# A gated long-convolution and token-mixer kernel on one core: spectral buffers laid out at equal steps, the filter's special row put last, a part of the first norm on ScalarE, a new order of the instructions

## The chip, the cores and the metric

The kernel runs on one core of one Trainium2 chip. A core has five engines that work side by side, each through its own instructions in order: TensorE (PE, matmuls, with weight loads shown as PEld), VectorE (DVE), ScalarE (ACT), GpSimd (POOL) and SyncE (SP). Here SP only issues transfers (DMAs), POOL issues some of them and computes a few reciprocal roots. Engines wait for each other by semaphores. The metric is the time of one execution on the device in microseconds (us), the median over several runs.

## The reference

All arrays are bf16. x is `A_q`, of 2048 tokens by 640 channels; k and v have the same shape.

```python
def _A_ref(q, k, v, shift_k, ssm_k, ssm_D):      # L = 2 * S
    k_shift = sum over t of k_pad[:, t:t + S] * shift_k[:, 3 - t]     # causal, four taps
    kv = k_shift * v
    y_f = rfft(kv padded to L) * rfft(ssm_k padded to L)
    y = irfft(y_f)[:, :S]
    return q * (y + kv * ssm_D)
def _B_ref(x, w1, w2, w3, w4):
    h = _gelu(_layernorm(x) @ w1)
    g0, g1, g2, g3 = quarters of h's channels, moved by +1, -1, +2, -2 tokens
    x1 = x + concat(g0, g1, g2, g3) @ w2
    return x1 + _gelu(_layernorm(x1) @ w3) @ w4            # w3: 640 x 1536
g = _sigmoid((x * gate_w).sum(-1))
return g * _A_ref(x, A_k, A_v, ...) + (1 - g) * _B_ref(x, w1, w2, w3, w4)
```

So there are two branches: a long convolution of every channel over 2048 tokens with a filter of 2048 taps (a circular one of length 4096, by a Fourier transform), and a mixer with two norms and four matrix products. A gate per token adds them.

## The kernel before, in words

**Recording, order, emission.** The kernel is written as functions that record operations (engine, what is read, what is written). `tt` (L661) is a DVE operation of two tensors, `ts` (L666) one of a tensor with scalars, `act` (L671) an ACT one, `mm` (L693) a chain of matmuls into one PSUM tile. Since such helpers record nearly everything, most instructions of the profile carry the helper's line. `scale` and `turn` (L678 to L686) choose between two engines for one operation: each call has a default, and a string `ON` of zeros and ones, one for each call, flips it. Which operation is issued when is not found by the program: `SEQUENCE` lists all 1163 operations by number in the order in which they are put into their engines' streams, and `PLACES` gives each of the 206 PSUM tiles its bank (there are 8). `emit` then derives the semaphore waits from what reads and writes the same memory. A stream is strictly in order: an instruction that waits holds up everything behind it on its engine.

**The convolution** works in five chunks of 128 channels, c = 0 to 4. The transform of length 4096 is split: tokens are laid out as n, 512 outer positions by matmul against fixed cosine and sine tables, and 4 blocks (b) of them that are combined as a short product of polynomials. For one chunk:

- `h_load`, `h_fold`: the filter is loaded, added to and subtracted from its own mirror (`add` and `sub`, 1024 elements a partition each), the skip weight `ssm_D` is added into the special element 0, and a DMA transpose ("T h") turns it by 128x128 blocks so that time lies on the partitions. `h_even`: sum and difference of its even part. Partition 0 holds a row that does not follow the rule of the others: two sums of one row on DVE and one scaled copy of one row correct it. `h_chunk`: the filter's spectrum, four matmul groups j = 0 to 3 into two PSUM banks each, each copied by ACT into the spectral buffer (`HF`).
- `k_load`, `v_load`: k and v come in by DMA transposes, so that channels lie on the partitions. `kv`: the four taps are scalings of k (2048 elements, by default 0, 1 and 3 on ACT and 2 on DVE), three shifted adds, the product with v, sum and difference with the mirror (a fold), and a DMA transpose ("T kv"). `kv2`: again sum and difference.
- `x_fwd`: the spectrum of kv, four groups j again, copied by ACT into `XF`. `combine`: two DVE operations across the blocks.
- `unit`: the product of the spectra, on DVE. Complex numbers are multiplied with three real products; `SX` is the sum of real and imaginary part of kv's spectrum, `HD` the sum and another buffer the difference for the filter's. For each output pair of blocks and each filter block a there is a product of 2 x 512 per block with two strides, another of 512 per block for the third, and an add into an accumulator. The sums of real and imaginary part (`Y`) are two subtractions or adds; a one-row copy fixes partition 0.
- `final(g, o, q, k)`: the inverse. Channels 0 to 383 are group 0 (chunks 0 to 2) and 384 to 639 group 1; there are eight calls of each, each for a pair of 128-token tiles. Two chains of matmuls, an ACT copy (`ab`), sum and difference on DVE (`gy`), a matmul against a flipped identity (`flip`) for the mirrored tile, its copy with the gate's weight, then product with q times gate, and the add to the mixer's output: group 0 by an accumulating DMA from POOL, group 1 by DVE from SBUF and a store by SP (64 KB stores for the last two calls of the function, 128 KB for the other six, in L1044 and after).

**The mixer** works in 16 tiles of 128 tokens, four to a superchunk (sc). `ln1`: mean and variance by DVE (`bn_stats`, L862, two halves a tile, and `bn_aggr`, L863) for tiles 0 to 9, by ACT (a sum and a sum of squares with an accumulator) for 10 to 15; a reciprocal root on POOL (L870); the application (subtract the mean, multiply) by DVE in all 16. Tiles 0 to 7 are then turned on PE (L923), the others by DMA transposes. `mm1` with gelu on ACT writes the hidden layer channels first; its fifth group of channels (`hx`) is moved by tokens in small copies on DVE or DMA (L947). `mm2` plus the residual is one DVE operation with an accumulated sum (L981), then ACT squares the tile for the second norm. `ln2` applies it (by default tiles 0 to 3 on DVE and the others on ACT), a DMA transpose follows. `mm3`, gelu, `mm4`; `base` scales half a tile by one minus the gate and stores it, and an accumulating DMA adds mm4's.

**What sets the order.** All streams interleave the two branches: PE goes from the first norm's transposes to mm1 of superchunks 0 to 2, chunk 0's filter matmuls (h, j = 0 to 3) between mm2 of the first tiles, and so on; the inverse comes last. Before the first real work PE runs 15 warm-up matmuls (L717) on a tile of ones, 512 columns each.

The five lines that place the first norm's split, which the change touches:

```python
PET, LNS, LNA = 8, 10, 4
...
            if t < LNS:
                ln_bn(t, X[:, t, :])
                continue
            act(xn1[t // 2 % 2][:, t % 2], X[:, t, :], ACTF.Copy, scale=1.0 / D, accum=bna[:, t, 0:1])
```

## Time and profile before

| | |
|---|---|
| median of 3 runs | 219.88 us (219.87 to 219.89) |
| span of the profiled execution | 218.0 us |
| PE busy | 208.8 us (96%) |
| PEld busy (lies beside PE) | 126.2 us (58%) |
| DVE busy | 211.7 us (97%) |
| ACT busy | 196.9 us (90%) |
| POOL busy | 46.5 us (21%) |
| DMA | 37.68 MB, mean 173 GB/s |

The profile is of one execution. Its span of 218.0 us runs from its first to its last instruction; what a run's time counts beyond that is the difference to the median, 1.9 us. A row of a group reads: line, engine, operation, what is written from what is read with the shape of each, how often, then busy time in all, mean nanoseconds of one, and idle time ahead of them with what ended most of it. A row of the timeline starts with its start and length in us; neighbours on one engine overlap a little, since an instruction starts before the one ahead has drained, so that the step from start to start is what one more instruction costs. Matmuls are pipelined too: a "busy" PE can also be one that waits for operands, so its busy share alone says little. "arena" is the one SBUF buffer in which the kernel places all its tiles.

### The profile page before, as it was taken

How to read it: one execution, taken by the hardware profiler on the slowest of the kernel's cores; microseconds unless marked ns; L12 is line 12 of the kernel's file. 1: busy time of each engine (PE TensorE's matmuls, PEld its weight loads, DVE VectorE, ACT ScalarE, POOL GpSimd, SP SyncE). 2: the span in 40 equal slices, each digit the busy share in tenths (PEclk: the TensorE clock that was granted, in tenths of full speed). 3: DMA queues.
4: the chain of work that ended last, by engine and by line, in shares of the span. 5: the costliest groups of instructions: out<-in, count | busy, mean ns of one | idle time of the engine just before them, and what ended most of it. 6: DMA issues, size and time to landing. Idle time of an engine off the chain costs nothing.

```text
span 218.0 us, 3825 instructions
## 1 busy us (share of the span) xinstructions
PE 208.8 (96%) x1400; PEld 126.2 (58%) x1410; DVE 211.7 (97%) x411; ACT 196.9 (90%) x328; POOL 46.5 (21%) x48
## 2 busy tenths in 40 slices
PE   6999999999999999999999999999999999999971
PEld 1699755554664446665446764446566445777740
DVE  5999999999999999999999999999999999999994
ACT  2699999999999999999999989999897977868882
POOL 0421103400001101000600301403004560256440
PEclk9999999999999999999999999999999999999995
DMA  5998799999999967999085684787289999069796
GB/s 158 348 242 224 182 220 226 219 202 246 298 228 197 353 172 150 191 195 203 29 162 99 123 201 96 71 180 126 72 123 164 176 206 265 5 74 103 80 165 136
DMA packets 79344, 37.68 MB, mean 173 GB/s; under 512 B 58969, under 2 KB 76894, under 8 KB 79326
## 3 DMA queue, kind: packets, MB, share of 16 engines
q1 hardware_dynamic: 73824, 31.86, 64.0%
q0 software_dynamic: 5328, 5.51, 19.1%
q8 instruction: 11, 0.18, 0.3%
q10 hardware_dynamic: 174, 0.07, 0.1%
q14 instruction: 7, 0.06, 0.1%
HBM read 14.88 MB, written 5.77 MB: 95 GB/s over the span
## 4 chain that ended last, share of the span: by engine, by line
PE 72%; DVE 17%; ACT 5%; DMA 3%; issue 2%
PE PSall L693 72%; DVE arena L661 8%; ACT arena L671 5%; DVE arena L862 4%; DVE arena L666 3%; DMA arena<-arena 2%; DVE arena L947 1%; DMA arena<-in_A_q_dram 1%; DVE arena L863 0%; DVE arena L737 0%; DVE arena L981 0%; DVE arena L867 0%
## 5 line engine op out<-in xcount | busy, mean ns | idle before, releaser
L693 PE MATMUL PSall<-arena 128*128 128x256 bf16 (+5 forms) x1339 | 201.1, 309 | 3.5 <-DVE arena L661 2.4
L661 DVE TENSOR_TENSOR arena<-arena 128x1024 bf16<-128x1024 bf16 (+11 forms) x264 | 174.3, 725 | 0.6
L693 PEld LDWEIGHTS PSall<-arena 128*128 128x128 bf16 x1349 | 121.9, 98 | 81.8 <-DVE arena L661 3.2
L671 ACT ACTIVATE arena<-PSall 128x512 bf16<-128x512 f32 (+7 forms) x158 | 94.9, 669 | 7.6 <-PE PSall L693 5.3
L671 ACT ACTIVATE arena<-arena 128x640 bf16<-128x640 bf16 (+6 forms) x107 | 94.1, 910 | 1.0 <-DMA arena<-arena 0.5
L870 POOL TENSOR_TENSOR arena<-arena 128x2 f32<-128x2 f32 (+2 forms) x15 | 17.6, 1174 | 92.9 <-DVE arena L867 78.2
L237 POOL DMA_DIRECT2D out_dram<-arena x24 | 24.7, 1235 | 37.6 <-ACT arena L671 19.8
L671 ACT ACTIVATE arena<-PSall,arena 128x640 bf16<-128x640 f32 (+2 forms) x32 | 20.6, 656 | 6.9 <-PE PSall L693 6.8
L981 DVE SCALAR_TENSOR_TENSOR arena<-PSall,arena 128x640 bf16<-128x640 f32 x16 | 13.0, 816 | 0.3 <-PE PSall L693 0.3
L237 POOL DMA_DIRECT2D arena<-arena x5 | 4.9, 988 | 35.5 <-DVE arena L661 28.4
L666 DVE TENSOR_SCALAR arena<-arena 128x640 bf16<-128x640 bf16 (+6 forms) x31 | 11.6, 385 | 0.1
L862 DVE BATCH_NORM_STATS2 arena<-arena 128x6 f32<-128x320 bf16 x20 | 8.6, 480 | 1.1 <-DMA arena<-in_A_q_dram 1.1
L717 PE MATMUL PSall<-arena 128*128 128x512 bf16 x15 | 6.7, 584 | 2.0 <-DVE arena L714 2.0
L947 DVE TENSOR_SCALAR arena<-arena 32x256 bf16<-32x256 bf16 (+1 forms) x24 | 5.8, 242 | 0.5
L671 ACT ACTIVATION_READ_ACCUMULATOR arena<-arena 128x1 f32 x28 | 6.2, 221 | 0.0
L717 PEld LDWEIGHTS PSall<-arena 128*128 128x128 bf16 x15 | 1.8, 129 | 4.2 <-issue 2.2
L923 PE MATMUL PSall<-arena 128*128 128x128 bf16 x40 | 3.5, 219 | 0.0
L671 ACT ACT_TABLE_LOAD x1 | 1.3, 1283 | 2.5 <-issue 2.5
L923 PEld LDWEIGHTS PSall<-arena 128*128 128x128 bf16 x40 | 2.8, 99 | 0.6 <-DVE arena L666 0.3
L867 DVE SCALAR_TENSOR_TENSOR arena<-arena 128x2 f32<-128x2 f32 (+2 forms) x19 | 2.8, 154 | 0.0
L863 DVE BATCH_NORM_AGGREGATE arena<-arena 128x2 f32<-128x12 f32 x10 | 1.7, 196 | 0.0
L981 DVE DVE_READ_ACCUMULATOR arena<-PSall,arena 128x1 f32 x16 | 1.3, 81 | 0.0
(21 smaller groups left out, 4.3 us busy)
## 6 DMA issues: line engine op xcount, KB each, us to landing
arena<-in_A_ssm_k_dram SPq DMA_DIRECT2D x5, 512.0 KB, 5.2
arena<-in_A_q_dram SPq DMA_DIRECT2D x6, 320.0 KB, 5.4
arena<-in_B_w_dram SPq DMA_DIRECT2D x1, 1920.0 KB, 9.0
out_dram<-arena SPq DMA_DIRECT2D x16, 96.0 KB, 2.5
arena<-arena POOLq DMA_DIRECT2D x4, 384.0 KB, 4.1
out_dram<-arena POOLq DMA_DIRECT2D x16, 96.0 KB, 4.5
arena<-in_A_q_dram SPq DMA_DIRECT2D x8, 192.0 KB, 4.0
out_dram<-arena POOLq DMA_DIRECT2D x8, 192.0 KB, 4.1
```

The source lines that it names most:

```text
L237: fn = lambda e: e.dma_start(out, in_, **kw)
L661: P.op(eng, lambda e: e.tensor_tensor(o, real(a), real(b), op), [a, b], [o], dve_ns(o, [a, b], 2) if eng == "dve" else 500)
L666: P.op(eng, lambda e: e.tensor_scalar(o, real(a), s1, s2, op0=op0, **({} if op1 is None else {"op1": op1})), [a] + aps, [o], dve_ns(o, [a] ...
L671: P.op("act", lambda e: e.activation(real(o), real(a), f, bias=bias, scale=scale, **({"accum_out": accum} if accum is not None else {})), ...
L693: fns.append(lambda e, l=l, r=r, i=i: e.matmul(real(o), l, r, start=(i == 0), stop=(i == last)))
L717: P.op("pe", lambda e: e.matmul(real(pw), warm[:, 0:128], warm[:, 128:640], start=True, stop=True), [warm], [pw], 427.0 if i < 14 else 216.0)
L862: P.op("dve", lambda e, o=o, i=i: e.bn_stats(o, i), [i], [o], 400)
L867: P.op("dve", lambda e: e.scalar_tensor_tensor(o, a, x, b, op0=op0, op1=op1), [a, b] + aps, [o], n_of(o) / 0.96 + 65)
L870: P.op("pool", lambda g: g.tensor_tensor(o, a, e, ALU.pow), [a, e], [o], dur)
L923: P.op("pe", [lambda e, c=c, pb=pb, xn=xn: e.transpose(real(pb)[:, 128 * c:128 * (c + 1)], xn[:, 128 * c:128 * (c + 1)], ident) for c in r ...
L947: P.op("dve", lambda e, o=hT[q, 4, c0:c0 + n], i=hx[q, :]: e.tensor_scalar(o, i, 1.0, None, op0=ALU.mult), [hx[q, :], hT[q, 4, c0 - 1:c0]] ...
L981: P.op("dve", lambda e: e.scalar_tensor_tensor(x, real(pr), 1.0, x, op0=ALU.mult, op1=ALU.add, accum_out=st[1, 0][:, t:t + 1]), [pr, x], [ ...
```

## The change

- **Spectral buffers at equal steps.** The real part, imaginary part and their sum of a chunk's spectrum (`oXr`, `oXi`, `oSX`) lie at one distance from each other, and the filter's difference, sum and real part (`oHm`, `oHP`, `oHr`) too. So the two sums SX and HP are one operation of 4096 elements, the two products of a step are one of 1536 per block (three strides), and the two halves of Y one subtraction.
- **The filter's special row last.** The tables are built so that the special element is the last of 128, not the first; `h_fold` writes plain blocks, and the two one-row sums and the one-row scaling of `h_even` are replaced by SP DMAs of one row: two copies in one operation, and a third that reads what the first writes. `copies` is new: several small DMAs counted on one semaphore.
- **First norm.** Statistics on ACT for tiles 1 and 10 to 15 (`SUMS`); application on ACT for 10 to 15 (`TURNS`), which needs one more small DVE operation (minus mean times root).
- **Unit's fix of one row.** A copy on ACT or two SP DMAs, by the switch.
- **Small things.** The warm-up reads one 128-column tile four times over instead of a 640-column one, its length in PSUM is the same; three small loads move from ACT's queue to POOL's; many buffers move; some constants of the planner's costs differ (they change no instruction).
- **New SEQUENCE, PLACES and ON.** There are now 1114 operations: DVE 352 instead of 395, ACT 283 instead of 302, SP 113 instead of 102, POOL 46 instead of 44, PE 320 as before. By the switches, ten instead of four taps run on DVE (0 and 1 of chunk 0; 0, 1 and 3 of chunk 1; 2 of chunk 0, 2 and 3; 0 and 3 of chunk 3; in chunks 1 and 4 tap 2 is on ACT), the second norm's application on DVE in tiles 0 to 3, 13 and 14, `base` on DVE in tiles 1, 2, 4, 12 and 14 instead of 5, and in the unit four adds instead of five go by DMA (u0 a=1, u1 a=2 and a=1, u2 a=1).

Some of what the new order puts where, since the prediction speaks of it:

- Loads of x on SP: tile 3, 0, 1, 2. On DVE: statistics of tiles 3 and 0, their aggregates, an epsilon of tile 3, the square of tile 1's mean (which reads ACT's sums), epsilon of tile 0, statistics of tile 2, variance of tile 1, application of tile 3, aggregate of tile 2, application of tile 0.
- ACT, a run of the stream: squares of tiles 2, 0, 3 (second norm), sums of 13 and 12 (first norm), square of 1, then 13, 15, 12, 14, a small copy, 15, 14, one gelu of hx (1024 tokens on), gelus of superchunk 2 groups 0 and 1, applications of tiles 13 and 12, gelus of groups 2 and 3, applications 14 and 15, then the copies of filter chunk 0, j = 0, 3, 2, 1, and the first forward copies.
- PE at that place: mm1 of superchunk 2, filter matmul c0 j = 2, 0, mm2 of tiles 7 and 9 in between, j = 3, and j = 1 into the bank of j = 3.
- SP in chunk 2: T h, load of w4, T of the second norm, the row's first two copies, T of the second norm, transpose of v, the row's last copy. The first PE user of the row is filter matmul c2 j = 3.
- DVE at the end: gy and ab sums, products and adds of the last calls of `final`; the last store on SP is the 128 KB one of call 5 in group 1.

```diff
+    def copies(self, queue, pairs):
+        fns = [lambda e, o=o, i=i: e.dma_start(o, i) for o, i in pairs]
+        op = Op(len(self.ops), queue, fns, [i for _, i in pairs], [o for o, _ in pairs], 470.0 * len(pairs), 0.0, 1024 * len(pairs))
+        op.cost = 10.0 * len(pairs)
+        op.lat = 2300.0
+        return self._record(op)
...
+    p = (np.arange(128)[:, None] + 1) % 128
...
+    xp = lambda i: oXF + U * (i + 2)
+    hp = lambda i: oHF + U * (i + 5)
+    XSTEP, HSTEP = (3, 4, 5, -1, 1), (1, 2, 3, 4, 5)
+    oXr, oXi = [xp(2 * i) for i in XSTEP], [xp(i) for i in XSTEP]
+    oHr, oHm = [hp(i) for i in HSTEP], [hp(-i) for i in HSTEP]
+    oSX, oHP, oTA, oRh = xp(0), hp(0), xp(7), xp(9)
...
-    P.op("dve", lambda e: e.memset(warm, 1.0), [], [warm], 230)
+    P.op("dve", lambda e: e.memset(warm, 1.0), [], [warm], 165)
+    wide = at_sb(oUT, (0, 4), (1, 128))
...
-    P.dma("act", shk5, A_shift_k.rearrange("(c p) j -> c (p j)", p=128))
+    P.dma("pool", shk5, A_shift_k.rearrange("(c p) j -> c (p j)", p=128))
...
     def h_even(c):
-
         ev, o = het[c], evn[c]
         tt(o[:, 0], ev[:, :, :, 0], ev[:, :, :, 1], ALU.add)
         tt(o[:, 1], ev[:, :, :, 0], ev[:, :, :, 1], ALU.subtract)
-        tt(o[0:1, 0, 0], ev[0:1, 1, :, 0], ev[0:1, 0, :, 0], ALU.add)
-        tt(o[0:1, 1, 0], ev[0:1, 1, :, 0], ev[0:1, 0, :, 0], ALU.subtract)
-        scale(o[0:1, :, 1], ev[0:1, :, :, 1], 1.0, True)
+        last = slice(127, 128)
+        P.copies(sp, [(ev[last, 1, :, 0], ev[last, 0, :, 0]), (ev[last, 1, :, 1], o[last, 1, 1])])
+        P.copies(sp, [(ev[last, 0, :, 0], o[last, 0, 1])])
...
-            if a >= LNS:
+            if a in SUMS:
                 tt(st[0, 4][:, a:b], mean, mean, ALU.mult)
                 stt(st[0, 3][:, a:b], st[0, 1][:, a:b], 1e-5, st[0, 4][:, a:b], ALU.add, ALU.subtract)
...
+            if a in TURNS:
+                stt(st[0, 6][:, a:b], mean, -1.0, st[0, 5][:, a:b], ALU.mult, ALU.mult)
...
+    SUMS, TURNS = (1, 10, 11, 12, 13, 14, 15), (10, 11, 12, 13, 14, 15)
...
-            ts(xn, x, bna[:, t, 0:1], st[0, 5][:, t:t + 1], ALU.subtract, ALU.mult)
+            if t in TURNS:
+                act(xn, x, ACTF.Identity, scale=st[0, 5][:, t:t + 1], bias=st[0, 6][:, t:t + 1])
+            else:
+                ts(xn, x, bna[:, t, 0:1], st[0, 5][:, t:t + 1], ALU.subtract, ALU.mult)
...
     def unit(c):
-        X4, H4 = XF[:, c], HF[c]
-        tt(SX, X4[:, :, 0], X4[:, :, 1], ALU.add)
-        tt(HD, H4[:, :, 0], H4[:, :, 1], ALU.add)
-        tt(H4[:, :, 1], H4[:, :, 1], H4[:, :, 0], ALU.subtract)
+        dx, dh = oXi[c] - oXr[c], oHP - oHm[c]
+        both = lambda x, h: at_sb(x, (h - x, 2), (1, U))
+        tt(both(oSX, oHP), both(oXr[c], oHr[c]), both(oXi[c], oHm[c]), ALU.add)
+        tt(V(oHm[c], U), V(oHr[c], U), V(oHm[c], U), ALU.subtract)
...
-                tt(to[:, :, 0:2], X4[:, x0:x0 + n], uv, ALU.mult)
-                tt(to[:, :, 2], SX[:, x0:x0 + n], H4[:, a, 0].unsqueeze(1).to_broadcast([128, n, 512]), ALU.mult)
+                tt(tmp if a else acc, at_sb(oXr[c] + 512 * (lo - a), (512, n), (dx, 3), (1, 512)),
+                   at_sb(oHm[c] + 512 * a, (0, n), (dh, 3), (1, 512)), ALU.mult)
...
-            tt(Y[:, :, 0], R[:, :, 2], R[:, :, 1], ALU.subtract)
-            tt(Y[:, :, 1], R[:, :, 2], R[:, :, 0], ALU.add)
-            scale(Y[0:1, :, :, 0:128], R[0:1, :, 0:2, 0:128], 1.0, True)
+            n = o1 - o0
+            tt(at_sb(oXr[c] + 512 * o0, (512, n), (dx, 2), (1, 512)), at_sb(oACC + 1024, (1536, n), (0, 2), (1, 512)),
+               at_sb(oACC + 512, (1536, n), (-512, 2), (1, 512)), ALU.subtract)
+            fix = lambda o, so, sr: bass.AP(AR[:, 0:16].tensor, o, [[part[0], 1], [so, n], [sr, 2], [1, 128]])
+            fo, fi = fix(oXr[c] + 512 * o0, 512, dx), fix(oACC, 1536, 512)
+            if turn(False):
+                P.copies(sp, [(fo[:, :, r], fi[:, :, r]) for r in range(2)])
+            else:
+                act(fo, fi, ACTF.Copy)
```

177 lines of the change are left out of this document (85 added, 92 removed), and 119 rows, old and new, of tables (PLACES, SEQUENCE).

## The prediction

> **What bounds the kernel now.** I read the page first (busy shares, slices), then the stretches by engine, then the groups by shape, then the timeline of each engine at three places.
>
> ```profile
> span 218.0 us, 3825 instructions
> PE 208.8 (96%) x1400; PEld 126.2 (58%) x1410; DVE 211.7 (97%) x411; ACT 196.9 (90%) x328; POOL 46.5 (21%) x48
> ```
>
> ```profile
> PE   6999999999999999999999999999999999999971
> ```
>
> ```profile
> DVE  5999999999999999999999999999999999999994
> ```
>
> ```profile
> 210.00:214.00 4.00, 1.57 (x11) 0.77 (x8) 4.00 (x16) 2.70 (x7) 1.20 (x1) 0.85 0.92 155
> ```
>
> The slices are tenths of 5.45 us each; the stretch from 210 to 214 us gives busy times of PE, PEld, DVE, ACT, POOL, then granted clock, DMA share and GB/s. PE and DVE are both full from 5 to 210 us; then PE runs dry and DVE does not. Is a full PE really working? The price of a matmul says so:
>
> ```profile
> L693 PE MATMUL PSall<-arena 128*128 128x512 bf16 x29 | 6.4, 379 | 0.0
> ```
>
> ```profile
> L693 PE MATMUL PSall<-arena 128*128 128x256 bf16 (+5 forms) x1339 | 201.1, 309 | 3.5 <-DVE arena L661 2.4
> ```
>
> ```profile
> 8.13 0.44 PE L923 MATMUL PSall<-arena 128*128 128x128 bf16 x5
> ```
>
> The first is the group row of 132 to 138 us: 0.22 us for 512 columns. The second is the page's row of all of this line, 201.1 us busy. The same by the price, in proportion to columns: 410 of 512, 264 of 384, 340 of 256, 160 of 320, 120 of 128 columns and 85 single ones make some 202 us. The third, of the timeline, is the first transpose, at 8.1 us; 202 from there end at 210. So PE loses about 1 us in 200, and its order cannot be fed late anywhere without moving the end. DVE is the second bound. Time by median is 219.88 us (219.87 to 219.89); the profiled execution has a span of 218.0, so I carry 1.9 us around it unchanged. Differences under 0.2% (0.44 us) I call no change.
>
> **The change, part by part.**
>
> *Work on each engine.* DVE prices:
>
> ```profile
> L661 DVE TENSOR_TENSOR arena<-arena 128x3072 bf16<-128x3072 bf16 x9 | 15.7, 1747 | 0.0
> L661 DVE TENSOR_TENSOR arena<-arena 128x1024 bf16<-128x1024 bf16 x89 | 58.2, 681 | 0.2
> L661 DVE TENSOR_TENSOR arena<-arena 128x2048 bf16<-128x2048 bf16 x39 | 47.0, 1214 | 0.1
> L661 DVE TENSOR_TENSOR arena<-arena 1x512 bf16<-1x512 bf16 x10 | 4.1, 405 | 0.0
> L666 DVE TENSOR_SCALAR arena<-arena 128x640 bf16<-128x640 bf16 x16 | 6.8, 428 | 0.0
> L666 DVE TENSOR_SCALAR arena<-arena 128x2048 bf16<-128x2048 bf16 x4 | 2.9, 748 | 0.0
> L671 ACT ACTIVATE arena<-arena 128x2048 bf16<-128x2048 bf16 x16 | 32.0, 2026 | 0.0
> L671 ACT ACTIVATE arena<-arena 1x1024 bf16<-1x1024 bf16 x4 | 4.2, 1039 | 0.0
> ```
>
> ```profile
> 3.44 1.67 DVE L862 BATCH_NORM_STATS2 arena<-arena 128x6 f32<-128x320 bf16 x4 [1.14 <-DMA arena<-in_A_q_dram]
> 5.03 0.33 DVE L863 BATCH_NORM_AGGREGATE arena<-arena 128x2 f32<-128x12 f32 x2
> ```
>
> 1024 and 2048 elements cost 681 + 1214 = 1895 ns apart and 1747 merged, of which neighbours overlap by some 80 ns: 0.07 us for each of 47 merges, -3.2. The ten 1-row sums of the filter go: -3.4 (0.405 less overlap). Six norm applications go to ACT, tile 1's statistics too (the two last rows: 0.42 each for two halves, 0.17 for the aggregate): -3.1. Against it the new switches put six more taps (0.67 each, +4.0), six second-norm applications (+2.1), six scalings of 0.2 and one add of 0.9 (+2.2) on DVE; small ones balance. Net about -2 us. ACT loses what these switches give DVE (six taps at 1.9, six applications, six scalings and an add) and the four filter copies at 1.0, and gains six first applications and some sums: about -17 us. PE keeps every matmul. Nothing of this shows unless PE's order is fed earlier; PE has only its front and its tail to give. The merged patterns I price as plain ones: today's product already walks two buffers by a stride at the price above. Its bounds are that price and, if merged, never under one of 2048.
>
> *The tail: -0.6 us.* Both orders end PE with equal work, so the last inverse is copied at the same moment, 210.79 + 0.60 = 211.4:
>
> ```profile
> 210.79 0.60 ACT L671 ACTIVATE arena<-PSall 128x512 bf16<-128x512 f32 x1
> ```
>
> ```profile
> 215.19 0.29 DVE arena L661
> ```
>
> ```profile
> L661 DVE TENSOR_TENSOR arena<-arena 128x512 bf16<-128x512 bf16 x17 | 6.9, 419 | 0.0
> L661 DVE TENSOR_TENSOR arena<-arena 128x256 bf16<-128x256 bf16 x24 | 6.3, 284 | 0.2
> ```
>
> Now DVE's last op ends at 215.5, after flips that PE does for it one by one. The new order has eleven DVE ops left (eight of 256 at 0.20 start to start, two of 512 at 0.34, one of 768 at 0.47): 2.8 us after 211.55, so 214.4, or 1.1 earlier. But its last store is of 128 KB instead of 64:
>
> ```profile
> out_dram<-arena SPq DMA_DIRECT2D x6, 128.0 KB, 2.6
> out_dram<-arena SPq DMA_DIRECT2D x4, 64.0 KB, 1.7
> ```
>
> 0 to 0.9 later; I take 0.5. Tail -0.6 (-1.1 to -0.2): 219.3 if nothing else happens.
>
> *Tile 1 of the first norm: DVE +1.2 us.* Its sums now come from ACT, and the product of means (m2 of tile 1) stands on DVE behind tiles 3 and 0 and ahead of tile 2's statistics. Tile 1 is the third load.
>
> ```profile
> 0.75 2.32 SPq L237 DMA_DIRECT2D arena<-in_A_q_dram  x5
> ```
>
> ```profile
> 0.75 2.66 DMA arena<-in_A_q_dram
> ```
>
> ```profile
> arena<-in_A_q_dram SPq DMA_DIRECT2D x4, 160.0 KB, 3.2
> ```
>
> ```profile
> 6.82 0.39 DVE L666 TENSOR_SCALAR arena<-arena 128x640 bf16<-128x640 bf16 x1
> ```
>
> ```profile
> 30.56 0.72 ACT L671 ACTIVATE arena<-arena 128x640 bf16<-128x640 bf16 x1
> 31.18 0.19 ACT L671 ACTIVATION_READ_ACCUMULATOR arena<-arena 128x1 f32 x1
> ```
>
> Five issues in 2.32 us put the third at 1.67. The first landed after 2.66 (a step of the chain of waits; DVE starts at 3.44 above); the median of four is 3.2, so with two near 2.6 the other two took some 3.8 and the third lands at 5.5. ACT's sum, by the same work at 30.56, adds 0.72 + 0.19, a signal 0.1: 6.5. DVE is there at 5.3 (four halves, two aggregates, one small op). Bounds: 0 if it lands with the median or before (4.9 gives +0.6), 1.4 at most. Taken 1.2. All DVE work queued behind, the other tiles' applications first (today's first is the row at 6.82), is late by that.
>
> *ACT's run at 29 to 46 us: PE +2.2 us.* Six applications are added to ACT just where it is full today:
>
> ```profile
> 32.00 0.58 ACT L671 ACTIVATE arena<-PSall 128x512 bf16<-128x512 f32 x1
> 32.47 0.72 ACT L671 ACTIVATE arena<-arena 128x640 bf16<-128x640 bf16 x1
> ```
>
> ```profile
> 45.33 0.94 ACT L671 ACTIVATE arena<-arena 128x640 bf16<-128x640 bf16 x1
> 46.14 1.96 ACT L671 ACTIVATE arena<-PSall 128x1024 bf16<-128x1024 f32 x2
> ```
>
> ```profile
> 26.70 0.81 DVE L981 SCALAR_TENSOR_TENSOR arena<-PSall,arena 128x640 bf16<-128x640 f32 x1
> ```
>
> Start to start: a sum or square 0.72 (30.56 to 31.28), a gelu of 512 0.47, a copy of 1024 0.90, an application 0.81. In the new order ACT's square of tile 2 waits for that DVE sum (x1 of tile 2, 26.70 today); ahead of it DVE has 0.8 more (in 3.3: chunk 1's fold 1.3, one tap 0.67, a filter sum 0.6, two shifts 0.5, three small; out 2.5) and the 1.2 above, so 28.7 + 0.8. From 29.5 ACT runs without a gap: 12 sums and squares 8.6, five gelus 2.4, four applications 3.2, a small copy, two filter copies 1.8 = 16.1, to 45.6. Chunk 0's filter matmul j1 takes the bank that the second of these copies frees: 45.8. PE by its own work is there earlier: 34.4 us of matmuls stand ahead of it (37 of 512, 85 of 320, 60 of 256, 120 of 128 columns, 60 single), from 8.1 and with the 0.8 lost by then today 43.4 to 43.6. PE +2.2; without the wait for tile 1 it would be 1.1. Six taps are gone from ACT, but later ones: in this run there is only one less.
>
> *The row copies by DMA: PE +0.3 us.* DVE then waits for the last forward copy of chunk 0 (52.5 against 49.6 by its own work) and is 3.0 late. Chunk 2's filter difference ends after 71.0 us of DVE work from 3.44: 74.4, with 3.0 at 77.4. Behind it on SP stand the first two copies, a transpose of the second norm, v of chunk 2, and the last copy, which waits for the first.
>
> ```profile
> 27.50 2.25 SPq L234 DMA_TRANSPOSE arena<-in_A_v_dram  x1
> ```
>
> ```profile
> 51.41 1.35 SPq L234 DMA_TRANSPOSE arena<-arena  x1
> ```
>
> 0.1, two issues of 0.46 as for the loads, 1.35 and 2.25 put the last issue at 82.0; landing after 1.7 (the 64 KB stores; nothing smaller is measured) at 83.7, and 0.2 for the signals. PE wants the row for filter matmul j3 with 72.2 us of work ahead, the same in both orders: 81.4 to 81.6, with 2.2 at 83.8. Taken +0.3; 0 at best, +0.9 if the copy lands only behind the transpose it follows.
>
> The Trainium skill (DMA: Bandwidth & Descriptors, Anatomy of one DMA — SWDGE (gpsimd) path) says that a DMA issued by GpSimd costs about 2.0 us of setup and completion whatever its size, which speaks against moving rows by two dependent ones. This trace's 64 KB stores from SP, at 1.7 in all, lie a little under it; no run here shows so small a copy yet. With 2.0 in place of 1.7 this term would be 0.6 (an estimate from the page).
>
> *Edits with one answer.* Warm-up from one 128-column tile, the three small loads on POOL, the row folded last, new banks: 0. What hides them is the wait of the first transpose for tile 3 (first application at 6.8 today, as above). If a POOL load lands after 7 us, PE's first transpose moves by the same, up to 1 us, still inside the 2.2.
>
> Sum: 219.9 - 0.6 + 2.2 + 0.3 = **221.8 us**.
>
> **The rivals.**
> - *Faster: the new order keeps PE full.* For it: DVE and ACT have less to do. Against: the full ACT row at 30 to 47 us. The place is filter matmul j1 of chunk 0; it decides if ACT gets there by 43.6, 2.2 earlier than counted. The tail alone is left then: 219.3 (218.8 to 219.7).
> - *ACT's run alone.* Tile 1 lands with the first loads; PE +1.1, copies +0.1: 220.5.
> - *The copies bound chunk 2.* The last copy lands behind v's transpose (+0.9), and that issues more slowly behind the load of w4 than at 27.50 (the chunk-2 row below): each us of that is a us of PE, so 222.4 and up; I let one us in, 223.4.
>
> ```profile
> 69.02 7.55 SPq L234 DMA_TRANSPOSE arena<-in_A_v_dram  x1
> ```
>
> - *The merge doesn't merge.* If the three-way patterns fell off the fast rate, 30 products would each cost over 1 us more and the time pass 240. Today's two-way stride at full price speaks against it.
>
> **How the numbers follow.** Forecast 0.46 (221.8, own range 221.2 to 222.4), ACT alone 0.14 (220.5; 0.02 of it so little late that it is no change), copies 0.08, PE kept full 0.30 (by the spread of its tail 0.22 faster, 0.08 no change), patterns 0.02. Range 218.8 to 223.4, from the faster rival to the copies, with the patterns left out. Faster 0.22, no change 0.10, slower 0.68.
>
> **What would show it.** Right: DVE idle about 1 us near 5.4 us for ACT; ACT without a gap from 29 to 46; PE idle or stretched by 2 us between 33 and 46 with ACT named; DVE near 209.5 busy and ACT near 180; merged products at 1.75 us. Wrong: PE full at 43 us, no DVE wait at 5 us, or the copies of chunk 2 landed well before PE asks.

## The result, and the profile after

The changed kernel takes 227.1 us (median of 4 runs, 226.38 to 228.17), the kernel before on the same chip 219.88 (219.87 to 220.12): a ratio of 1.0325 (95% interval 1.0295 to 1.0355), 7.2 us slower. The forecast was 221.8 us with a range of 218.8 to 223.4: the sign was right, the time far outside. The profiled execution took 227.14 us with a span of 225.3, so 1.8 us lie around the span (1.9 before).

The page of the changed kernel, its busy shares and two rows of its slices (a slice is now 5.63 us):

```profile
span 225.3 us, 3792 instructions
...
PE 210.9 (94%) x1410; PEld 124.3 (55%) x1410; DVE 211.2 (94%) x368; ACT 181.4 (80%) x313; POOL 49.5 (22%) x50
...
PE   6699999999999999999999999999999999999960
...
DVE  4899999989999999899889999999989999999991
```

PE's row still reads 9 nearly everywhere: its "busy" hides waiting for operands, as the prediction warned. DVE's row tells more: where it was 9 from the second slice to the 39th, five slices in the middle of the run are now 8. The page's chain of waits, by engine, after and then before:

```profile
DVE 49%; PE 22%; DMA 9%; ACT 9%; issue 4%; POOL 3%; SPq 1%; DVEq 0%
```

```profile
PE 72%; DVE 17%; ACT 5%; DMA 3%; issue 2%
```

PE carried the chain of the old kernel; DVE carries that of the new one. The stretches show the same, busy time of PE, PEld, DVE, ACT and POOL in each, then granted clock, DMA share and GB/s; first the kernel before, then after:

```profile
17.00:43.00 26.00, 25.73 (x223) 17.42 (x222) 25.48 (x72) 25.52 (x58) 6.38 (x5) 1.00 0.99 210
43.00:62.00 19.00, 18.78 (x124) 10.45 (x125) 18.86 (x38) 18.75 (x27) 0.00 (x0) 1.00 1.07 256
62.00:106.00 44.00, 43.90 (x252) 24.59 (x253) 43.67 (x62) 43.77 (x61) 4.89 (x3) 1.00 0.92 199
106.00:128.00 22.00, 21.87 (x131) 13.02 (x133) 21.93 (x34) 21.81 (x32) 3.64 (x4) 1.00 0.64 117
128.00:205.00 77.00, 76.87 (x469) 45.95 (x471) 76.85 (x118) 67.94 (x106) 23.87 (x24) 1.00 0.73 129
```

```profile
17.00:43.00 26.00, 24.55 (x207) 16.23 (x208) 25.53 (x73) 23.40 (x59) 6.18 (x5) 1.00 1.12 226
43.00:62.00 19.00, 19.00 (x129) 10.83 (x128) 17.81 (x37) 17.98 (x23) 0.00 (x0) 1.00 0.96 206
62.00:106.00 44.00, 43.02 (x248) 23.53 (x247) 43.10 (x60) 42.95 (x68) 7.06 (x5) 1.00 1.03 224
106.00:128.00 22.00, 21.31 (x108) 9.82 (x107) 20.46 (x26) 18.17 (x30) 8.96 (x7) 1.00 0.95 193
128.00:205.00 77.00, 76.68 (x461) 44.70 (x462) 75.98 (x78) 55.55 (x81) 15.16 (x16) 1.00 0.52 92
```

From 43 to 205 us DVE was idle for 0.7 us before and for 4.7 after. The clock is 1.00 in all of them, so no part of the loss in these stretches is the clock's.

To place the loss, take for each group of matmuls its start in the trace less the work that stands ahead of it in PE's order (by the prices of the prediction, counted from 8.1 us, where the old kernel's first transpose starts). This lateness of PE was about 0.8 us before up to 42 us and 0.95 at the end. After:

| start of the matmul, us | 10 | 17 | 27 | 33 | 42 | 63 | 80 | 106 | 128 | 168 | end |
|---|---|---|---|---|---|---|---|---|---|---|---|
| PE late by, us | 0.8 | 1.1 | 1.7 | 2.5 | 3.35 | 4.0 | 4.6 | 5.3 | 6.7 | 7.4 | 7.5 |

So up to the filter matmuls at 42 us PE loses 2.55 us, and then another 3.7 to 4.0 in small pieces, spread over 160 us. PE's own waits in the changed kernel (what it waits for; us in total, times, longest), first from 8 to 43 us, then from 43 to 205:

```profile
PE PSall L696 <- DMA arena<-in_B_w_dram: 1.0, 2, 0.6
PE PSall L696 <- ACT arena L674: 0.8, 2, 0.4
PE PSall L696 <- DVE arena L987: 0.6, 2, 0.4
PE PSall L929 <- DVE arena L669: 0.2, 1, 0.2
```

```profile
PE PSall L696 <- ACT arena L674: 0.8, 3, 0.3
PE PSall L696 <- DVE arena L987: 0.4, 1, 0.4
PE PSall L696 <- DVE arena L664: 0.3, 1, 0.3
```

The same view of the old kernel from 43 to 205 us has no line. The view leaves out the shortest waits, so these 1.5 us are less than the 3.7 to 4.0. The last inverse's copies end 6.3 us later than before. At the end DVE needs 3.1 us behind them instead of 4.1, but the span ends 4.6 us after DVE's last instruction instead of 2.5. Together: 6.3 - 1.0 + 2.1 = 7.4; the two spans differ by 7.3.

The rows that the prediction named as its marks, of the changed kernel's timeline (start, length, instruction, and in brackets the idle time ahead with what ended it), DVE's wait for tile 1, ACT's run, and PE behind it:

```profile
5.90 0.16 DVE L664 TENSOR_TENSOR arena<-arena 128x1 f32<-128x1 f32 x1 [0.57 <-ACT arena L674]
```

```profile
29.96 0.74 ACT L674 ACTIVATE arena<-arena 128x640 bf16<-128x640 bf16 x1 [0.73 <-DVE arena L987]
...
44.35 2.84 ACT L674 ACTIVATE arena<-PSall 128x1024 bf16<-128x1024 f32 x3
47.65 1.02 ACT L674 ACTIVATE arena<-PSall 128x1024 bf16<-128x1024 f32 x1 [0.47 <-PE PSall L696]
```

```profile
42.41 19.99 PE L696 MATMUL PSall<-arena 128*128 128x512 bf16 x131 [0.41 <-ACT arena L674]
```

DVE waits for ACT at 5.3 us, but 0.57 and not 1.2. ACT runs from 29.96 to 47.2 without a bracket, that is without a gap. PE's filter group of chunk 0 is let go by ACT. The merged operations, from the groups by shape:

```profile
L664 DVE TENSOR_TENSOR arena<-arena 128x3072 bf16<-128x3072 bf16 x28 | 48.9, 1753 | 0.3 <-DMA arena<-arena 0.2
L664 DVE TENSOR_TENSOR arena<-arena 128x4096 bf16<-128x4096 bf16 x5 | 11.4, 2283 | 0.0
```

The three-stride product takes 1753 ns, as the plain one of that size did (1747). The prediction has no line for these idle times of DVE, in its timeline:

```profile
91.21 0.16 DVE L867 SCALAR_TENSOR_TENSOR arena<-arena 128x4 f32<-128x4 f32 x1 [0.90 <-POOL arena L870]
109.47 0.16 DVE L867 SCALAR_TENSOR_TENSOR arena<-arena 128x2 f32<-128x2 f32 x1 [0.61 <-POOL arena L870]
113.68 0.16 DVE L867 SCALAR_TENSOR_TENSOR arena<-arena 128x2 f32<-128x2 f32 x1 [0.58 <-POOL arena L870]
164.32 21.60 DVE L664 TENSOR_TENSOR arena<-arena 128x2048 bf16<-128x2048 bf16 x27 [0.69 <-DMA arena<-arena]
```

Three waits for the second norm's reciprocal roots on POOL (2.1 us in all) and two for an add that a DMA makes in the unit (0.9 in all). The old kernel has none of these waits.

### The profile page after: what moved, and what is told of

Read it like the earlier page. It is cut to its first block, busy times and chain, and to the rows that moved or that the text cites. A ratio compares the mean times of both kernels' runs of the same rounds, so it can differ in the third digit from the quotient of the medians.

```text
span 225.3 us, 3792 instructions
## 1 busy us (share of the span) xinstructions
PE 210.9 (94%) x1410; PEld 124.3 (55%) x1410; DVE 211.2 (94%) x368; ACT 181.4 (80%) x313; POOL 49.5 (22%) x50
## 4 chain that ended last, share of the span: by engine, by line
DVE 49%; PE 22%; DMA 9%; ACT 9%; issue 4%; POOL 3%; SPq 1%; DVEq 0%
DVE arena L664 42%; PE PSall L696 22%; ACT arena L674 9%; DMA arena<-arena 6%; DMA arena<-in_B_w_dram 3%; POOL arena L870 3%; DVE arena L669 3%; DVE arena L987 2%; DVE arena L953 2%; SPq L237 1%; DVE arena L867 0%; DVE arena L862 0%; DVEq L1151 0%; PE PSall L929 0%; DVE arena L863 0%
## 5 line engine op out<-in xcount | busy, mean ns | idle before, releaser
L696 PE MATMUL PSall<-arena 128*128 128x512 bf16 (+5 forms) x1349 | 204.0, 309 | 5.3 <-ACT arena L674 1.6
L664 DVE TENSOR_TENSOR arena<-arena 128x1024 bf16<-128x1024 bf16 (+11 forms) x209 | 170.1, 871 | 2.3 <-DMA arena<-arena 0.9
L696 PEld LDWEIGHTS PSall<-arena 128*128 128x128 bf16 x1349 | 120.4, 98 | 88.1 <-ACT arena L674 9.6
L674 ACT ACTIVATE arena<-arena 128x640 bf16<-128x640 bf16 (+5 forms) x92 | 75.8, 848 | 8.8 <-DMA arena<-in_A_q_dram 3.4
L870 POOL TENSOR_TENSOR arena<-arena 128x2 f32<-128x2 f32 (+2 forms) x15 | 20.3, 1378 | 74.6 <-DVE arena L867 61.7
L669 DVE TENSOR_SCALAR arena<-arena 128x640 bf16<-128x640 bf16 (+6 forms) x41 | 17.5, 433 | 0.2
L862 DVE BATCH_NORM_STATS2 arena<-arena 128x6 f32<-128x320 bf16 x18 | 7.9, 480 | 2.5 <-DMA arena<-in_A_q_dram 2.5
L237 POOL DMA_DIRECT2D arena<-arena x4 | 3.9, 975 | 27.7 <-DVE arena L664 20.2
L721 PE MATMUL PSall<-arena 128*128 128x512 bf16 x15 | 5.3, 491 | 1.1 <-DVE arena L717 1.1
L867 DVE SCALAR_TENSOR_TENSOR arena<-arena 128x2 f32<-128x2 f32 (+3 forms) x23 | 3.5, 160 | 2.2 <-POOL arena L870 2.1
L721 PEld LDWEIGHTS PSall<-arena 128*128 128x128 bf16 x15 | 1.6, 120 | 3.2 <-issue 1.9
L929 PEld LDWEIGHTS PSall<-arena 128*128 128x128 bf16 x40 | 2.5, 97 | 1.0 <-DVE arena L669 0.7
```

The source lines that it names most:

```text
L237: fn = lambda e: e.dma_start(out, in_, **kw)
L664: P.op(eng, lambda e: e.tensor_tensor(o, real(a), real(b), op), [a, b], [o], dve_ns(o, [a, b], 2) if eng == "dve" else 500)
L669: P.op(eng, lambda e: e.tensor_scalar(o, real(a), s1, s2, op0=op0, **({} if op1 is None else {"op1": op1})), [a] + aps, [o], (dve_ns(o, [a ...
L674: P.op("act", lambda e: e.activation(real(o), real(a), f, bias=bias, scale=scale, **({"accum_out": accum} if accum is not None else {})), ...
L696: fns.append(lambda e, l=l, r=r, i=i: e.matmul(real(o), l, r, start=(i == 0), stop=(i == last)))
L721: P.op("pe", lambda e: e.matmul(real(pw), warm, wide, start=True, stop=True), [warm], [pw], 216.0)
```

## The experiments

Every run lists its median against the kernel before on the same chip. "PE earlier by" compares the start of the same matmul in two traces. The first microseconds differ from run to run by 0.3 to 1.2 us with no change there (the small loads, x and the first weights land sooner or later), so a shift counts only where it arises behind that. Two base kernels are used: the changed one, with one part undone, and the old one, with one part added. In the experiments' kernels the helpers have other line numbers: there L610 to L614 is `tt`, L642 to L646 `mm`, L620 to L624 `act`.

**The late roots replaced (no_late_roots).**

```diff
-        pool_pow(s[5], s[3], neghalf[:, a:b])
+        (ts(s[5], s[3], 1.0, None, ALU.mult) if l == 1 and a >= 8 else pool_pow(s[5], s[3], neghalf[:, a:b]))
```

> Changed kernel, with the reciprocal root of the second norm for tiles 8 to 15 (three POOL operations) replaced by a copy of the same few elements on DVE; the root itself is left out, so those tiles' norm is not the reference's. Theory A (DVE waits for POOL's roots and everything behind it is late): the three waits of 0.90, 0.61 and 0.58 us vanish for 0.2 us of copies, 227.1 - 1.9 = 225.2. Rival B (the waits lie in slack of a stage that PE or ACT sets): 226.8 to 227.3.

225.67 us, ratio 1.0266 (1.0245 to 1.0287). Compared with the changed kernel PE is 0.8 earlier from its first groups on, which this edit doesn't touch, stays there up to 95 us, and is 1.3 earlier at 105 and 1.7 to 2.0 from 119 us to the end. So the roots are worth 1.0 us, half of the 2.1 that DVE waited. The rest turned up elsewhere: DVE's wait for the DMA's adds grew from 0.9 to 1.6 us.

**The roots left on POOL, but with DVE work moved ahead of what reads them (roots_moved).** Moved on DVE, by names:

```diff
-root of tiles 8 to 11 is read; ...; fold of kv, chunk 2 (add, sub)
+fold of kv, chunk 2 (add, sub); root of tiles 8 to 11 is read
-root of tiles 14, 15 is read; ...; unit, a product of o = 1
+unit, a product of o = 1; root of tiles 14, 15 is read
-root of tiles 12, 13 is read; ...; an add and sub of the filter, chunk 3
+an add and sub of the filter, chunk 3; root of tiles 12, 13 is read
```

> Changed kernel; on DVE the two folds of kv in chunk 2 go ahead of the operation that needs the root of tiles 8 to 11, one product of unit 1 ahead of that of tiles 14 and 15, and a shifted add ahead of that of tiles 12 and 13. If POOL gets in between two DVE operations, the three waits vanish: -1.0, as without the roots. If POOL stands still as long as DVE issues operations of two SBUF inputs, the waits only move, and the time is the same or up to 1 more.

226.97 us, 1.0306 (1.0289 to 1.0322). The waits of this kernel (engine and line, what it waits for; us in total, times, longest):

```profile
DVE arena L614 <- DMA arena<-arena: 1.4, 2, 0.9
DVE arena L614 <- ACT arena L624: 1.0, 2, 0.8
...
DVE arena L817 <- POOL arena L820: 0.6, 1, 0.6
```

The wait for roots fell from 2.1 to 0.6, those for DMA and ACT rose by 0.5 and 0.3 (in the changed kernel 0.9 and 0.7), and PE ended where it did in the changed kernel (0.06 later). It had begun up to 0.6 later, but that was gone by 27 us (0.02), ahead of everything that was moved. So nothing is gained at PE: the wait moved, it did not vanish.

**The DMA's adds on DVE (adds_dve).** Two of the unit's adds go back to DVE, the code's default, by their switches.

> Changed kernel, with two of the unit's adds that went by accumulating DMA back on DVE (unit 1 block 2 a=1, 3072 elements, 1.7 us; unit 2 block 0 a=1, 1536 elements, 0.9). DVE's waits for them (0.2 and 0.7) go, 2.6 of work comes: +1.7 if DVE sets the time at both places; if their landing also delays the other DMAs that PE or ACT wait for, less, down to 0.

229.0 us, 1.0395 (1.0376 to 1.0414); PE is 1.2 to 1.5 later from 115 us on. The two adds cost DVE 2.6 us of work, the waits they save are 0.9, and most of the difference arrives at PE. DVE sets the pace there.

**The merged operations split again, all else as changed (split).**

```diff
-        tt(both(oSX, oHP), both(oXr[c], oHr[c]), both(oXi[c], oHm[c]), ALU.add)
+        many([both(oSX, oHP), both(oXr[c], oHr[c]), both(oXi[c], oHm[c])], ALU.add, lambda v: [v[:, 0], v[:, 1]])
...
-                tt(tmp if a else acc, at_sb(oXr[c] + 512 * (lo - a), (512, n), (dx, 3), (1, 512)),
-                   at_sb(oHm[c] + 512 * a, (0, n), (dh, 3), (1, 512)), ALU.mult)
+                many([tmp if a else acc, at_sb(oXr[c] + 512 * (lo - a), (512, n), (dx, 3), (1, 512)),
+                      at_sb(oHm[c] + 512 * a, (0, n), (dh, 3), (1, 512))], ALU.mult, lambda v: [v[:, :, 0:2], v[:, :, 2]])
```

> Changed kernel, with every merged operation of the unit issued as two instructions in the same place of the order (product: two strides and one; the two sums; the two halves of Y). Theory A (DVE is full and sets the time from 53 to 168 us): 46 more instructions at 0.07 each, +3.2, so 229.5 to 230.5. Rival C (long merged instructions hold POOL's roots and transfers back, and splitting frees them): the roots of 2.8 and 4.0 us shrink to under 2 and the time rises by less than 1.5, or falls.

229.27 us, 1.0429 (1.0405 to 1.0454). 47 instructions more (DVE x415 instead of x368), PE 3.3 us later at the end: 0.07 each, the prediction's price for a merge to the digit. The waits for roots stay at 2.1. So the merging helps this order and is not what made it slow.

**The merged products and halves of Y in the old order (merge_products).** The old kernel with the new buffers, the product of three strides and the one subtraction; everything else (order, banks, switches, norm, row, loads) as before.

```diff
-                tt(to[:, :, 0:2], X4[:, x0:x0 + n], uv, ALU.mult)
-                tt(to[:, :, 2], SX[:, x0:x0 + n], H4[:, a, 0].unsqueeze(1).to_broadcast([128, n, 512]), ALU.mult)
+                tt(tmp if a else acc, at_sb(oXr[c] + 512 * (lo - a), (512, n), (dx, 3), (1, 512)),
+                   at_sb(oHm[c] + 512 * a, (0, n), (dh, 3), (1, 512)), ALU.mult)
...
-            tt(Y[:, :, 0], R[:, :, 2], R[:, :, 1], ALU.subtract)
-            tt(Y[:, :, 1], R[:, :, 2], R[:, :, 0], ALU.add)
+            tt(at_sb(oXr[c] + 512 * o0, (512, n), (dx, 2), (1, 512)), at_sb(oACC + 1024, (1536, n), (0, 2), (1, 512)),
+               at_sb(oACC + 512, (1536, n), (-512, 2), (1, 512)), ALU.subtract)
```

> As merge_old_order (old order, banks, switches, norm's split, row treatment, loads), but only the products and the two halves of Y are merged; the three sums of each unit stay single operations where the kernel before had them, and group 0 of the inverse has five result buffers in turn again instead of six. The two places where merge_old_order lost time were a merged pair of sums that had to stand where the later of the two stood (DVE 1.9 late at chunk 1's forward matmul j0, PE 1.1 later), and a DVE wait of 3.3 for the transfer of call 1 whose buffer call 7 took over. Theory F (the new order, not the new operations, costs the time): both go, 218.5 to 220.0. Rival C (merged operations slow the rest): 221 or more.

220.36 us against 220.27: ratio 1.0007 (0.9996 to 1.0018), no change. Its waits and a stretch of it:

```profile
DVE arena L610 <- ACT arena L620: 2.3, 5, 0.9
```

```profile
106.00:205.00 99.00, 99.00 (x604) 58.87 (x603) 96.33 (x118) 89.84 (x137) 27.95 (x28) 1.00 0.71 126
```

DVE saves 2.6 us of work in the whole run (busy 209.1 instead of 211.7) and is idle for 2.7 of the 99 us in which it had been idle for 0.2 (the two stretches of the kernel before above). PE stays within 0.4 us of the kernel before to the end. The new operation by itself changes nothing in this order, where PE is the bound.

**The sums merged too, in the old order (merge_old_order, then merge_all_old).** To merge two sums, both must stand where the later one stood. The first edit is on merge_products (in chunk 2 the two sums stay two instructions); the last two lines are all in which the second kernel differs from the first:

```diff
-        tt(V(oSX, U), V(oXr[c], U), V(oXi[c], U), ALU.add)
-        tt(V(oHP, U), V(oHr[c], U), V(oHm[c], U), ALU.add)
+        tt(both(oSX, oHP), both(oXr[c], oHr[c]), both(oXi[c], oHm[c]), ALU.add)
...
-        qt, gy, ab = (qA, qB)[g][k], (gyA[k % 6], gyB[k])[g], (abA[k % 4], abB[k])[g]
+        qt, gy, ab = (qA, qB)[g][k], (gyA[k % 5], gyB[k])[g], (abA[k % 4], abB[k])[g]
```

> The changed kernel's spectral buffers and merged operations, but the order, the banks, the switches, the norm's split, the row treatment (one-row sums on DVE) and the queue of the three small loads of the kernel before; one of the five merged pairs of sums stays two instructions. Theory A (the merge is worth its 3 us only where DVE sets the time; in the old order PE loses just 0.9 us and DVE's tail is set by PE's flips): PE's lateness shrinks from 0.95 to 0.5, 218.8 to 219.7. Rival C (the merged operations themselves are what slows the changed kernel, by long holds of POOL or by slow patterns): 221 or more.

> As merge_products, with the two sums of each unit merged too, at the place of the later one (merge_old_order with five result buffers for group 0). If that place is what made DVE 1.9 late and PE 1.1 at chunk 1's forward matmul j0: 221.2 to 221.8. If only the buffer cost time: 219.8 to 220.5.

225.77 us, 1.0245 (1.0214 to 1.0276), and 221.62 us, 1.007 (1.0057 to 1.0083). The first had a fault of transplanting: with six rotating buffers in this order DVE waited at 208 us for a store that still read its buffer.

```profile
DVE arena L610 <- DMA out_dram<-arena: 3.3, 1, 3.3
```

Without it, PE is level with merge_products up to 80 us, 0.3 later from there, and 1.4 later from 86 us to the end: two sums of chunk 1 that stood apart now stand together, and PE's second wave of forward matmuls waits, by way of ACT's copies, for DVE's work behind them. A merge that saves 0.07 us of work can cost over 1 us of place.

**The new norm split in the old order (norm_old_order).** merge_products plus one more line:

```diff
-    SUMS, TURNS = (10, 11, 12, 13, 14, 15), ()
+    SUMS, TURNS = (1, 10, 11, 12, 13, 14, 15), (10, 11, 12, 13, 14, 15)
```

> As merge_products (old order, merged products), with the changed kernel's split of the first norm: tile 1's statistics and the applications of tiles 10 to 15 on ACT, at the places of the order where DVE had them. By the prediction's term (six applications of 0.81 in ACT's full stretch from 29 to 46 us): PE 1.1 to 2.2 later at chunk 0's filter matmuls, 221.5 to 222.8. Rival (ACT takes them up, and DVE, 2 us lighter, hands PE its inputs sooner): 219.8 to 220.6.

228.26 us, 1.0359 (1.0333 to 1.0386). Its waits:

```profile
DVE arena L610 <- ACT arena L620: 5.2, 8, 1.6
PE PSall L642 <- ACT arena L620: 4.3, 6, 1.1
...
DVE arena L902 <- ACT arena L620: 3.2, 2, 2.0
```

PE is 0.8 us later than before at the first transposes and 2.5 at 11 us (tile 1: DVE waits for ACT's sums), still 2.5 at 25, then 5.3 at 30, 6.5 at 39 and 8.3 at 49 us (the applications, while ACT is full), and it stays there to the end. Of the parts put into the old order this is the heaviest: it costs 8 us there. In the new order the same two parts are worth far less, as the next two runs show. The two causes were not run apart in the old order; that they are two is read from when the lateness grows.

**Tile 1's statistics back on DVE, in the new order (tile1_dve).**

```diff
-    SUMS, TURNS = (1, 10, 11, 12, 13, 14, 15), (10, 11, 12, 13, 14, 15)
+    SUMS, TURNS = (10, 11, 12, 13, 14, 15), (10, 11, 12, 13, 14, 15)
```

> Changed kernel, with tile 1's statistics back on DVE (two halves, an aggregate, an epsilon) right behind tiles 3 and 0, nothing else. By the prediction's term (tile 1 on ACT makes DVE 1.2 us late, PE 1.1 later) it gains 0.8 to 1.1: 226.0 to 226.3. By the trace after (the wait is 0.57, the two small operations 0.2, against 1.1 of work for tile 1 on DVE) DVE is 0.3 later with tile 1: 227.1 to 227.5.

226.44 us, 1.0292 (1.0269 to 1.0316). PE is 0.87 earlier at 11 us and 0.68 to 0.76 from there to the end; no_late_roots, without this edit, had 0.8 at the same place. Tile 1 is worth 0.1 us or less here, not 1.2.

**The applications back on DVE, in the new order (turns_dve).**

```diff
-    SUMS, TURNS = (1, 10, 11, 12, 13, 14, 15), (10, 11, 12, 13, 14, 15)
+    SUMS, TURNS = (1, 10, 11, 12, 13, 14, 15), ()
```

> Changed kernel, with the first norm's application for tiles 10 to 15 back on DVE (and the three small products that it needed gone), the order else the same. Theory A (ACT's run from 29 to 47 us, and its wait of 1.7 for the root of tile 8 ahead of it, set PE's lateness up to 43 us): PE comes 1.0 to 1.5 us earlier to chunk 0's filter matmul j0, DVE has 1.9 more to do (six of 0.36 less three of 0.08), and the time goes to 226.0 to 227.0. Rival E (DVE's own lateness sets that place): PE later by 1 us or more there, 228 to 229.

228.19 us, 1.036 (1.0341 to 1.0379). PE is 0.68 earlier from its first groups to 25 us, 0.12 from 30 to 41, 0.70 and 0.86 earlier at the filter matmuls of chunk 0 (42 and 47 us), and 1.24 later at 49 us and 1.15 to 1.26 from there on. Waits of PE:

```profile
PE PSall L646 <- DVE arena L937: 4.0, 5, 1.9
```

With six instructions fewer on ACT the filter matmuls start only up to 0.2 us sooner, because DVE, which now has them, is late with the residual (L937 here) that comes first. In this stretch the six applications have no free engine: with them on ACT PE is seen to wait for ACT, and with them on DVE it waits for DVE and is later still.

**The small loads back on ACT's queue (loads_act).** The three loads are also issued ahead of ACT's table load again.

```diff
-    P.dma("pool", shk5, A_shift_k.rearrange("(c p) j -> c (p j)", p=128))
+    P.dma("act", shk5, A_shift_k.rearrange("(c p) j -> c (p j)", p=128))
...
-    P.dma("pool", dg5[:, 0:128], A_ssm_D.rearrange("(c p) -> c p", p=128))
+    P.dma("act", dg5[:, 0:128], A_ssm_D.rearrange("(c p) -> c p", p=128))
```

> Changed kernel, with the three small loads (shift_k, ssm_D, gate_w) issued by ACT again, ahead of its table load, as before the change. If their landing by POOL (PE's second small matmul waited between 0.4 and 2.0 us for ssm_D in the profiles so far) sets PE's start, that wait goes, PE reaches chunk 0's filter matmul 0.5 to 0.8 earlier, the times of single runs lie within 0.6 of each other, and the median is 226.0 to 226.5. If the loads of w1 set it anyway: 226.8 to 227.3, with the same spread.

226.65 us, 1.029 (1.027 to 1.0311). PE's wait for `ssm_D` (0.4 to 2.0 us in the runs with POOL) is gone, a wait of 0.7 for the first weights takes its place. PE is 0.4 earlier from 11 us on and 0.3 at the end, no more than the first microseconds differ by without such an edit: a gain is not shown.

**Without the row copies (no_row_copies).**

```diff
-        P.copies(sp, [(ev[last, 1, :, 0], ev[last, 0, :, 0]), (ev[last, 1, :, 1], o[last, 1, 1])])
-        P.copies(sp, [(ev[last, 0, :, 0], o[last, 0, 1])])
```

> Changed kernel without the small DMAs that repair the filter's last row (the spectrum of the filter is wrong in that row; their issues, waits and landings are gone from SP). By the prediction's term: -0.3. By the trace after (PE waits nowhere for them): 0, 226.8 to 227.4. Rival D (what is queued behind them on SP comes late, and that is the loss from 43 us on): -1.5 or more, under 225.6.

226.85 us, 1.032 (1.0295 to 1.0344). PE is 0.32 earlier from 27 us on and 0.41 at the end, and gains nothing at the filter matmuls that read the row. The copies cost nothing that shows.

**Without the last accumulating store (no_acc7).**

```diff
-            P.dma("pool", rows(out, 0, n), gy, accum=True)
+            if k < 7:
+                P.dma("pool", rows(out, 0, n), gy, accum=True)
```

> Changed kernel without the last accumulating transfer (384 KB, group 0, call 7; its rows of the output lack the convolution). If it is what makes the last stores land after 3.4 instead of 1.9 us, they land by 222.7 and the end comes 1.3 to 1.6 earlier. If the stores are slow by themselves (128 KB, two at a time): 0 to -0.3.

225.01 us, 1.0209 (1.019 to 1.0228). The transfer left out has 192 KB, not the 384 of the expectation. The profiled execution of this kernel had begun late, PE's last flips and DVE's end were 1.1 us later than in the changed kernel, and yet its span is 224.6, 0.7 shorter: the end behind DVE is 1.8 us shorter. The last issue on POOL in the changed kernel, then the median landing of the 64 KB stores from 205 us on, with that accumulation and without:

```profile
219.35 1.19 POOL L237 DMA_DIRECT2D out_dram<-arena  x1 [2.10 <-DVE arena L664]
```

```profile
out_dram<-arena SPq DMA_DIRECT2D x4, 64.0 KB, 2.3
```

```profile
out_dram<-arena SPq DMA_DIRECT2D x4, 64.0 KB, 1.5
```

The new order issues the last accumulation of group 0 at 219.35 us, 1.4 us before DVE's last instruction ends (220.73); it lands at 223.8, and the last two stores, issued at 220.42 and 220.82, land beside it after 3.55 and 3.37 us, at 224.0 and 224.2. In the old order the last accumulation is issued at 211.55, 4.0 us before DVE's end, and lands with it; the last two stores land after 1.94 and 1.53 us.

**The tail rearranged in the old order (tail_early).** merge_products with the flips of the last calls earlier on PE, and DVE's second halves of calls 6 and 7 ahead of call 4's:

```diff
-flips in the order of the calls, each behind its sum
+flips of calls 6 and 7 right behind that of call 5, their differences first on DVE
```

> As merge_products; only the last stretch differs: the differences of calls 6 and 7 (group 1) stand right behind their sums on DVE, their flips go ahead of call 4's on PE, and call 4 is finished last. If the flips that PE does one by one set the end: 0.5 to 1.0 less, 219.4 to 219.9, below the kernel before. If DVE's work sets it (it runs without a gap from 198 to 216): 220.2 to 220.6.

220.84 us, 1.0037 (1.0024 to 1.0051); 0.5 of it is a later start. Of the last three flips two came 1.2 and 1.4 us earlier than in merge_products and the third 0.5, and yet DVE ended 0.9 later (216.68 us against 215.79): what is left after the last copy is DVE's own work, not the way through PE.

**Three suspects out at once (three_off):** the late roots replaced, the last accumulation left out, the loads on ACT.

> Changed kernel with three single edits together: no late roots (a copy on DVE), the small loads on ACT, no last accumulating transfer. If their effects add (-1.0, -0.4, -1.9): 223.6 to 224.2, and some 4 us of the loss are neither of these but lie in the order. If they share one cause: 224.5 or more.

The times of this kernel scatter from 224.94 to 233.9 us (median 231.93; ratio by its two quickest runs 1.0269, 1.0223 to 1.0315), so whether the single effects add up can't be read. The profiled execution, one of 230.65 us, has a wait that no other trace shows:

```profile
123.57 1.76 DVE L614 TENSOR_TENSOR arena<-arena 128x3072 bf16<-128x3072 bf16 x1 [6.13 <-DMA arena<-arena]
```

An add of the unit, issued on POOL at 110.1 us with two accumulating stores directly behind it, landed 13.4 us later; in the nine other traces that have this add, of the changed kernel and its variants, it took 8.2 to 8.4. The two stores do not explain it: in no_late_roots they are issued as closely behind the add, and it took 8.3. Why it landed so late here, and whether the quicker runs have this wait, is not shown.

No kernel tried is faster than the kernel before; the best, merge_products, equals it.

## Why the prediction was wrong, step by step

- **Work on each engine.** The prices held (1753 ns for the merged product, 0.07 us for each merge by split). The sum did not: DVE is busy for 0.5 us less, not 2. The terms named in the prediction give -1.4 themselves; the "small ones" that it let balance cost the rest. Seen from the time this is minor. On PE two small errors cancel: the old trace lacks ten matmul records (x1400 against x1410 weight loads), so there are 420 matmuls of 512 columns and not 410, but the step from start to start is 0.216 us and not 0.22, and the sum of some 202 stands.
- **Tile 1, +1.2 on DVE.** The place was right, the size too large: 0.57 in the profile, and at most 0.1 of it at PE by tile1_dve. I had let the third load land at 5.5 us; it landed at 5.0.
- **ACT's run, PE +2.2.** The run was right: without a gap from 29.96 us, the second filter copy ending at 46.28 and filter matmul j = 1 starting at 46.33 (forecast 29.5, 45.6 and 45.8). What PE loses by it was read wrongly, and that 2.55 lies near 2.2 is in part luck. PE was to come on time and to lose the 2.2 at j = 1; it stands there for 0.1 at most, because it is late already. Of its waits from 8 to 43 us 1.0 is for the loads of w1 (at 9.3 and 10.6 us; 0.3 in no_late_roots, none in no_row_copies, so this part varies from run to run), 0.8 for DVE, and 0.8 for ACT, half of that ahead of the run. And 1.1 of the 2.2 hung on tile 1, which is worth 0.1. turns_dve adds that the applications have no free engine here: with them on DVE PE is later still.
- **Row copies, +0.3.** Nothing that shows, by no_row_copies.
- **The tail, -0.6.** DVE's part was right in size (forecast 1.1 earlier, measured 1.0), though by tail_early it isn't PE's flips that hold DVE at the end. The stores were mis-sized: I priced one store of 128 KB for one of 64 (+0.5) and looked at SP's queue alone. The accumulation that POOL issues beside them made it 2.1; no_acc7 takes 1.8 of it away. So the tail is +1.1 instead of -0.6. Each queue had to be followed to its end here, POOL's too.
- **The step that failed: "PE's order cannot be fed late anywhere without moving the end", and then a sum with no term between 46 us and the tail.** The sentence was right and I did not apply it. 3.7 to 4.0 us of PE's lateness arise between 43 and 205 us, where the sum has 0.3. In the old order DVE had not one wait there for POOL, ACT or a DMA (0.7 us idle in 162), and PE waited only 2.6 us in all for DVE's operations behind its front, 2.4 of it for the last three flips; I took that for a property of the work, but it was one of the order that was being replaced. With the merges and the switches every producer stands at another distance from its reader. What the runs give to the places: the late roots 1.0 us of PE (no_late_roots); the adds by DMA 0.9 of DVE's waits, which can't be taken out without giving DVE 2.6 of work (adds_dve); and in the old order a mere merging of sums 1.4 (merge_all_old). How the remaining 2 us divide among bank waits, DMA adds and merged sums in the new order stays open: where one wait is taken out, others grow, as no_late_roots and roots_moved show. In the terms of the sum: PE up to 42 us 2.55 instead of 2.2, the copies 0 instead of 0.3, the stretch behind 3.75 instead of nothing, the tail 1.1 instead of -0.6; 7.4 us instead of 1.9.

Of the rivals none came true. The faster one fell at the place it named, PE at 43 us; the one where the merge doesn't merge fell by the row of 1753 ns. A rival "DVE waits in the new order at places with no wait before, and PE follows" was missing. A bound for it was at hand: in the old kernel's trace POOL's root at 104 us took 2.5 us beside DVE work, and nothing in a new order promised that cover.

```profile
104.11 2.52 POOL L870 TENSOR_TENSOR arena<-arena 128x4 f32<-128x4 f32 x1 [20.76 <-DVE arena L867]
```

DVE read it 3.6 us after asking in the old order (13.9 for the longest), and after 2.1 to 4.2 in the new.

## What to carry to other kernels

Where two engines are full in the same order, a merged instruction saves only what the next reader can use: here 2.6 us of DVE work bought nothing in the old order, and a merge that moved one sum to the other's place cost 1.4. When a whole order is replaced, a wait of zero in the old trace is no evidence for the new one: take each producer with a long or uneven latency (a root on POOL, an add by DMA, a store that shares the engines) and count what stands between it and its reader in the new stream. And at the end of a kernel follow every queue to its last landing, also those of engines that have long been idle.

## What the runs showed of the hardware that I had not expected

**POOL's small root beside DVE.** The same kind of instruction in the changed kernel, first beside DVE's statistics (6.04 to 6.92 us), then beside two-tensor operations:

```profile
6.20 0.56 POOL L870 TENSOR_TENSOR arena<-arena 128x1 f32<-128x1 f32 x1 [0.21 <-DVE arena L669]
...
88.39 2.79 POOL L870 TENSOR_TENSOR arena<-arena 128x4 f32<-128x4 f32 x1 [17.71 <-DVE arena L867]
...
105.48 3.96 POOL L870 TENSOR_TENSOR arena<-arena 128x2 f32<-128x2 f32 x1 [1.61 <-DVE arena L867]
```

The two-tensor operations of DVE from 88.23 and 105.98 us end at 90.32 and 108.86, and the roots 0.86 and 0.58 later: DVE first makes POOL wait, then waits for it. The Trainium skill (SBUF — State Buffer, Who interferes with whom) states that a DVE instruction with two SBUF inputs contends with a GpSimd instruction that reads SBUF, and calls the shared ports an exclusive lock. The trace agrees in these rows. A row of such DVE operations does not shut POOL out for good: the old kernel's root above ended at 106.63 us, in the middle of a row of three such operations that lasts to 107.6, so a waiting POOL instruction can get in between two of DVE's.

**Adds and accumulations by DMA.** The unit's four adds by DMA took 3.9 to 8.2 us to land in the changed kernel, three of 384 KB and one of 768. The one of 768 KB took 8.2 to 8.4 in nine traces and 13.4 in one, and why is open. The stores of 64 KB beside a last accumulation took 2.3 us in the median, without it 1.5. In a tight order the landing of a transfer that adds has to be planned with room.
